# Cosine attention and a gated MLP on one core: AV turned round in batches 0 and 1, weights in larger packets, transfers held by waits

## The chip, the cores and the metric

The kernel runs on one core of a Trainium2 chip. Its metric is the device time of one execution in microseconds (us). A core has five engines that run their own instruction queues and meet through semaphores: TensorE (PE in the profile, with weight loads as PEld), VectorE (DVE), ScalarE (ACT), GpSimd (POOL) and SyncE (SP). Transfers are issued from the queues of SP, ACT and POOL and run on 16 DMA engines.

## The reference

Eight batches of 12 heads, 448 positions, head dimension 64, then an MLP from 768 over 2048 to 768 on the 3584 tokens; all in float32 at the kernel's borders.

```python
q_n = q / (norm(q) + 1e-6);  k_n = k / (norm(k) + 1e-6)
scores = q_n @ k_n.T / tau                       # tau = 0.1
attn = exp(scores - max(scores));  attn /= sum(attn) + 1e-9
x = (attn @ v) -> [tokens, heads * dim]
h = x @ w_in
out = (h * sigmoid(1.702 * h)) @ w_out
```

## The kernel before, in words

Heads go in pairs x: pair x belongs to batch x // 6, so that 0 to 5 are batch 0 and 6 to 11 batch 1; 48 pairs in all. Positions lie as 112 partitions by 4 chunks. For each pair q, k and v are loaded by SP (`load`, line 186, three transfers of 224 KB with 1 KB packets), ACT squares q and k (`square`, 193), DVE adds the squares up (`reduce`, 199) and turns the sums of a group of pairs into reciprocal norms (`norm_a`, `norm_b`, 212 to 240), POOL multiplies q and k with them and casts to fp16 (`scale`, 249), and v is cast with a column of ones beside it that makes the softmax denominators (`cast_v`, 262 or 264).

q and k must then lie with the head dimension on partitions. In batch 0 TensorE transposes them into PSUM and DVE copies them out (`transposes`, 271; `transposed`, 280); in the other batches a DMA transpose on SP does it (`dma_transposed`, 285).

Scores come with keys on partitions and queries along the row (`scores`, 297, and `scores_h`, 345, for half of the queries), ACT takes exp (`exp`, 308). AV has v as the stationary operand, with queries along the row and head dimension plus denominator on partitions (`attend`, 316; `attend_h`, 357). In batches 1 to 7 DVE evicts it (`attended`, 333), and for three pairs at a time the denominators go through DRAM to 112 partitions, are inverted on DVE (435), and come back spread over 64 partitions (`den_out` 423, `den_in` 430, `rcp_out` 440, `rcp_in` 445), for `normalise` (456). These transfers are issued by SP, but in batch 1 by ACT (`den_q`). Batch 0 takes halves of the queries instead: ACT evicts AV (`attended_h`, 367), TensorE picks the denominators onto partitions (`den_turn`, 375), DVE inverts them (386), TensorE spreads them (`den_spread`, 392), and DVE multiplies (`normalise_h`, 406).

The MLP of a batch starts when its six pairs are normalised: products with w_in (`mm1`, 467; for the halves of batch 0 `mm1_h`, 497), tanh on ACT (477), the gate on DVE (484; 509), products with w_out (`mm2`, 522), eviction on ACT (533), stores by SP (550). w_in and w_out come by two transfers each from POOL, which cast to fp16: w_in in halves of the columns (`load_w_in`, 558: 4 KB packets read), w_out in halves of the columns, too (`load_w_out`, 564: 1.5 KB packets read).

The order on each engine is not written by hand. Each step is an operation with an engine, an estimated duration, a due time, the operations it follows, and slots that it takes and frees (buffers, PSUM banks, and a "port" that keeps POOL apart from some DVE steps). `Plan.order` simulates the engines and the transfers with these and takes, on an idle engine, the ready operation that is due first; the instructions are issued in the order found. The semaphore waits come from the data alone. The due time of pair x is x in batch 0 and 2 x later. Loads of batch 1 follow scores or AV of batch 0 in the plan, w_in follows the load of q of pair 5, and w_out follows w_in. Slots: five q and five k buffers, three of v, one PSUM bank "a" (transposes and AV), two double banks for scores, three "mm" banks (MLP, and the denominators of batch 0).

Of the kernel before, what the change touches and what calls it, by code (L numbers as in the profile page):

```python
# [24 lines left out]
DMA_BYTES_PER_US = 250e3  # L25
MOE_FROM, MOE_LAG = 8, 9


class Plan:
# [3 lines left out]
    def __init__(self, slots):  # L33
        self.ops, self.free = {}, dict(slots)

    def add(self, name, eng, us, due, emit, after=(), takes=(), frees=(), nbytes=None, rows=128):
        self.ops[name] = (eng, us, due, emit, after, takes, frees, nbytes, rows)

    def order(self):
        ops = list(self.ops.values())  # L40
# [14 lines left out]
        while True:  # L55
            for e in idle:
                held = []
                while idle[e] <= now and ready[e]:
                    due, i = heapq.heappop(ready[e])
                    _, us, _, emit, _, takes, _, nbytes, rows = ops[i]  # L60
# [11 lines left out]
                    if nbytes is None:  # L72
                        heapq.heappush(events, (idle[e] + SEM_US, i, False))
# [5 lines left out]
            while True:  # L79
                heads = [q[0] for q in lines.values() if q]  # L80
                rate = DMA_BYTES_PER_US / max(len(heads), 1)
                landed = moved + min((h[0] for h in heads), default=0.0) / rate if heads else None
                if landed is None or (events and events[0][0] <= landed):
                    break
                for h in heads:
                    h[0] -= (landed - moved) * rate
                moved = landed
                for q in lines.values():
                    if q and q[0][0] <= 1e-3:
                        heapq.heappush(events, (moved + DMA_US + SEM_US, q.pop(0)[1], False))  # L90
# [3 lines left out]
            for h in heads:  # L94
                h[0] -= (now - moved) * rate
            moved = now
            while events and events[0][0] <= now:
                _, i, own = heapq.heappop(events)
                eng, nbytes = ops[i][0], ops[i][7]
                if own and nbytes is not None:  # L100
                    lines.setdefault(eng, []).append([nbytes, i])
                for s, k in ops[i][6]:
                    if own == (s == "port"):
                        self.free[s] += k
                for u in users[i]:
                    if (ops[u][0] == eng and nbytes is None) != own:
# [7 lines left out]
def kernel(  # L114
# [20 lines left out]
    NV = 6  # L135
    SH = S // 2
# [13 lines left out]
    p_in = pool("p_in", 5)  # L150
    p_v = pool("p_v", 3)
# [6 lines left out]
    p_ah = pool("p_ah", 2)  # L158
# [15 lines left out]
    pick = const.tile([128, 2], FP16)  # L174
# [8 lines left out]
    def load(x, d, src, nm):  # L183
        b, h0 = x // HP, (x % HP) * 2
        d[x] = p_in.tile([P, 2, C, D], FP32, name=nm)
        nc.sync.dma_start(
# [3 lines left out]

    def square(x, ti):
        sqs[x, ti] = p_sq.tile([P, 2, C, D], FP32, name="sq")
        nc.scalar.activation(out=sqs[x, ti], in_=(q32, k32)[ti][x], func=AF.Square)  # L193
# [39 lines left out]
    def norm_b(grp):  # L233
# [6 lines left out]
        nc.vector.tensor_tensor(out=y, in0=y, in1=t, op=ALU.mult)  # L240
# [4 lines left out]
    def scale(x, ti, eng=None):  # L245
# [3 lines left out]
        (eng or nc.gpsimd).tensor_tensor(  # L249
# [6 lines left out]
    def cast_v(x):  # L256
        src = v32.pop(x)
        vt = vts[x % NV]
        for j in range(2):
            dst = vt[:, :, j, 64 * j : 64 * j + D]  # L260
            if x < HP:
                nc.scalar.copy(out=dst, in_=src[:, j])
            else:
                nc.gpsimd.tensor_copy(out=dst, in_=src[:, j])  # L264
# [26 lines left out]
    tpss, exps, avs, sps, avps = {}, {}, {}, {}, {}  # L291
# [60 lines left out]

    def attend_h(x, h):
        ps = avps[x, h] = ps_a.tile([128, 2, SH], FP32, name="avh", tag="a")
        for j in range(2):
            for c in range(C):
                nc.tensor.matmul(  # L357
                    out=ps[:, j],
                    lhsT=vts[x % NV][:, c, j],
                    rhs=exps[x, h, c // 2][:, j, (c % 2) * SH : (c % 2 + 1) * SH],  # L360
                    start=(c == 0),
                    stop=(c == C - 1),
                )

    def attended_h(x, h):
        avs[x, h] = p_ah.tile([128, 2, SH], FP16, name="avsh")
        nc.scalar.activation(
            out=avs[x, h], in_=avps.pop((x, h)), func=AF.Copy, scale=AV_SCALE
        )

    def den_turn(x, h):
        ps = dps[x, h] = ps_m.tile([128, 512], FP32, name="mm")
        for i in range(2):
            for j in range(2):
                nc.tensor.matmul(
                    out=ps[:P, 2 * i + j : 2 * i + j + 1],
                    lhsT=avs[x, h][:, j, i * P : (i + 1) * P],
                    rhs=pick[:, j : j + 1],
                    start=True,
                    stop=True,  # L380
                )

    def den_rcp_h(x, h):
        r = dnms[x, h] = p_rc.tile([P, 4], FP16, name="rch")
        with nc.allow_low_precision("fp16 reciprocal of softmax denom"):
            nc.vector.reciprocal(out=r, in_=dps[x, h][:P, :4])

    def den_spread(x, h):
        r = dnms.pop((x, h))
        for i in range(2):  # L390
            for j in range(2):
                nc.tensor.matmul(
                    out=dps[x, h][64 * j : 64 * (j + 1), 64 + i * P : 64 + (i + 1) * P],
                    lhsT=r[:, 2 * i + j : 2 * i + j + 1].to_broadcast((P, 64)),
                    rhs=ident[:P, :P],
                    start=True,
# [399 lines left out]
```

## Time and profile before

| | |
|---|---|
| median of 3 runs | 505.68 us (505.25 to 506.33) |
| profiled execution | 505.82 us, of it the profile's span 503.9 us |
| TensorE busy | 464.0 us, 92% of the span, 2768 matmuls |
| ACT busy | 315.8 us, 63% |
| DVE busy | 279.2 us, 55% |
| POOL busy | 132.8 us, 26% |
| moved by DMA | 65.51 MB in 89902 packets, mean 130 GB/s |

The share of busy time is a mean over stages with different limits, and a matmul's busy time is longer when the clock granted to TensorE is lower. So a stage is read by its own windows: busy time of each engine, the granted clock beside it, and what the wait was for. The chain that ended last is the sequence of work that set the end, each piece with its start and length; where it passes from one engine to a DMA and back, the engines stood.

### The profile page before, as it was taken

The numbers are of one execution on the slowest core, as the hardware profiler recorded it, in microseconds if no ns is written. First come the engines' busy times: TensorE is split into PE (matmuls) and PEld (weight loads), VectorE is DVE, ScalarE is ACT, GpSimd is POOL, SyncE is SP. The second block draws the span as 40 slices with busy tenths as digits, with TensorE's granted clock in tenths as the row PEclk, the third lists the DMA queues.
The fourth block names the chain that finished last, engine by engine and source line by source line (L and its number), as shares of the span: only waits on it lengthen the run. The fifth ranks groups of instructions, "written<-read, shape, count | busy, mean of one in ns | idle before, by whom it ended". The sixth has DMA issues, their size and how long they took to land.

```text
span 503.9 us, 7803 instructions
## 1 busy us (share of the span) xinstructions
PE 464.0 (92%) x2768; PEld 248.1 (49%) x2768; DVE 279.2 (55%) x656; ACT 315.8 (63%) x497; POOL 132.8 (26%) x189
## 2 busy tenths in 40 slices
PE   0789889579699999999999999999999999999996
PEld 0566668325244455544544455445544554455553
DVE  7856476155476755396647745685468413641500
ACT  5968577283669765787668756786677545533411
POOL 1540525023426150515051505142503300000000
PEclk9999999858799999999999999999999999999999
DMA  9993819949268536755665365917570513012012
GB/s 225 237 234 103 205 34 156 223 116 224 62 181 196 152 68 188 150 163 97 183 166 145 73 154 141 243 36 201 132 178 24 132 33 91 2 60 64 0 40 86
DMA packets 89902, 65.51 MB, mean 130 GB/s; under 512 B 46388, under 2 KB 83080, under 8 KB 89864
## 3 DMA queue, kind: packets, MB, share of 16 engines
q1 hardware_dynamic: 83312, 58.02, 46.2%
q0 software_dynamic: 5696, 6.29, 7.8%
q10 hardware_dynamic: 856, 0.72, 0.5%
q8 instruction: 21, 0.34, 0.3%
q14 instruction: 17, 0.14, 0.1%
HBM read 50.51 MB, written 11.16 MB: 122 GB/s over the span
## 4 chain that ended last, share of the span: by engine, by line
PE 74%; DVE 7%; DMA 7%; ACT 5%; issue 3%; SPq 1%; POOL 1%; ACTq 0%; POOLq 0%; DVEq 0%
PE mm L522 26%; PE mm L467 22%; PE avp L316 11%; PE sp L297 6%; DMA q<-in_q_dram 3%; PE avh L357 3%; PE mm L497 3%; ACT expT L308 2%; PE sp L345 2%; DMA k<-in_k_dram 2%; ACT sq L193 1%; DMA den<-av 1%; DVE n L199 1%; DVE xT L456 1%; POOL qks L249 1%
## 5 line engine op out<-in xcount | busy, mean ns | idle before, releaser
L308 ACT ACTIVATE expT<-sp 112x896 f16<-112x896 f32 x192 | 166.5, 915 | 65.5 <-PE sp L297 57.4
L522 PE MATMUL mm<-w_out,gT 128*128 128x384 f16 x896 | 154.4, 329 | 0.0
L467 PE MATMUL mm<-xT,w_in 128*128 128x448 f16 x672 | 134.3, 353 | 1.2 <-DVE gT L484 1.1
L522 PEld LDWEIGHTS <-gT 128*128 128x128 f16 x896 | 85.6, 98 | 66.5 <-issue 13.0
L484 DVE SCALAR_TENSOR_TENSOR gT<-th,mm 128x448 f16<-128x448 f16 x112 | 67.9, 618 | 57.1 <-ACT th L477 56.6
L477 ACT ACTIVATE th<-mm 128x448 f16<-128x448 f32 x128 | 69.1, 545 | 45.8 <-PE mm L467 29.7
L467 PEld LDWEIGHTS <-w_in 128*128 128x128 f16 x672 | 63.0, 98 | 67.8 <-issue 13.0
L249 POOL TENSOR_TENSOR qks<-k,y 112x512 f16<-112x512 f32 x48 | 50.5, 1053 | 146.2 <-issue 101.6
L333 DVE TENSOR_SCALAR av<-avp 65x448 f16<-65x448 f32 x84 | 51.9, 618 | 62.6 <-PE avp L316 62.5
L316 PE MATMUL avp<-expT,vt 112*128 112x448 f16 x336 | 82.0, 366 | 1.6 <-DVE av L333 1.3
L199 DVE TENSOR_REDUCE n<-sq 112x8 f32<-112x512 f32 x96 | 63.7, 679 | 29.9 <-ACT sq L193 29.5
L297 PE MATMUL sp<-qkT 64*112 64x448 f16 x336 | 54.3, 388 | 13.7 <-ACT expT L308 13.6
L264 POOL CAST vt<-v 112x256 f16<-112x256 f32 x84 | 32.4, 417 | 116.9 <-DMA v<-in_v_dram 99.0
L533 ACT ACTIVATE ost<-mm 128x384 f32<-128x384 f32 x56 | 27.3, 490 | 51.9 <-PE mm L522 50.4
L249 POOL TENSOR_TENSOR qks<-q,y 112x512 f16<-112x512 f32 x47 | 49.0, 1042 | 0.0
L316 PEld LDWEIGHTS <-vt 112*128 112x128 f16 x336 | 32.7, 99 | 32.9 <-issue 6.7
L297 PEld LDWEIGHTS <-qkT 64*112 64x112 f16 x336 | 17.1, 129 | 49.7 <-issue 47.1
L456 DVE TENSOR_TENSOR xT<-av,rcb 64x448 f16<-64x448 f16 x84 | 34.5, 411 | 7.0 <-DMA rcb<-rcp 5.7
L193 ACT ACTIVATE sq<-k 112x512 f32<-112x512 f32 x48 | 30.2, 630 | 10.6 <-DMA k<-in_k_dram 6.6
L193 ACT ACTIVATE sq<-q 112x512 f32<-112x512 f32 x48 | 30.3, 632 | 2.9 <-DVE n L199 1.6
L497 PE MATMUL mm<-xT,w_in 128*128 128x224 f16 x192 | 21.7, 273 | 0.0
L497 PEld LDWEIGHTS <-w_in 128*128 128x128 f16 x192 | 19.1, 104 | 2.4 <-issue 1.6
(41 smaller groups left out, 171.4 us busy)
## 6 DMA issues: line engine op xcount, KB each, us to landing
k<-in_k_dram SPq DMA_DIRECT2D x48, 224.0 KB
q<-in_q_dram SPq DMA_DIRECT2D x48, 224.0 KB
v<-in_v_dram SPq DMA_DIRECT2D x48, 224.0 KB
rcb<-rcp SPq DMA_DIRECT2D x24, 168.0 KB
w_in<-in_moe_w_in_dram POOLq DMA_DIRECT2D x2, 1536.0 KB, 17.4
w_out<-in_moe_w_out_dram POOLq DMA_DIRECT2D x2, 1536.0 KB, 21.4
out_dram<-ost SPq DMA_DIRECT2D x7, 336.0 KB
out_dram<-ost SPq DMA_DIRECT2D x8, 288.0 KB
```

The lines of the kernel that those rows point to most:

```text
L193: nc.scalar.activation(out=sqs[x, ti], in_=(q32, k32)[ti][x], func=AF.Square)
L199: nc.vector.tensor_reduce(out=n2s[grp][:, x - grp[0], ti], in_=sqs.pop((x, ti)), axis=AX.X, op=ALU.add,)
L249: (eng or nc.gpsimd).tensor_tensor(out=qkss[x][:, ti].rearrange("p c j d -> p j c d"), in0=src, in1=rss[x][:, ti, :, :, None].to_broadcast ...
L297: nc.tensor.matmul(out=sp[:, j, :S], lhsT=qkT[64 * j : 64 * (j + 1), 1, c * P : (c + 1) * P], rhs=qkT[64 * j : 64 * (j + 1), 0, :], start= ...
L308: nc.scalar.activation(out=e, in_=sps.pop(key)[:, :, :S], func=AF.Exp, scale=inv_tau, **kw)
L316: nc.tensor.matmul(out=ps, lhsT=vts[x % NV][:, c, j], rhs=exps[x, c][:, j], start=(c == 0), stop=(c == C - 1),)
L333: nc.vector.tensor_scalar(out=avs[x][:n, j], in0=ps[:n], scalar1=AV_SCALE, scalar2=None, op0=ALU.mult)
L467: nc.tensor.matmul(out=ps[:, :S], lhsT=w_in_sb[:, kk, 128 * m : 128 * (m + 1)], rhs=xTs[b, kk], start=(kk == 0), stop=(kk == KT1 - 1),)
L477: nc.scalar.activation(out=ths[key], in_=mms[key][:, :S], func=AF.Tanh, scale=0.851)
L484: nc.vector.scalar_tensor_tensor(out=gts[b // 2][:, m, (b % 2) * S : (b % 2 + 1) * S], in0=ths.pop((b, m)), scalar=1.0, in1=mms.pop((b, m) ...
L497: nc.tensor.matmul(out=ps[:, i * SH : (i + 1) * SH], lhsT=w_in_sb[:, kk, 128 * (m + i) : 128 * (m + i + 1)], rhs=xTs[0, kk][:, h * SH : (h ...
L522: nc.tensor.matmul(out=mms[b2, t, n][:, :NW], lhsT=gts[b2][:, kk, 128 * t : 128 * (t + 1)], rhs=w_out_sb[:, kk, NW * n : NW * (n + 1)], st ...
```

## The change

In batches 0 and 1 the exponentials become the stationary operand of AV and v the moving one, so that queries lie on partitions and the denominator is a column; DVE inverts and multiplies there, TensorE transposes the result back, and a copy (ACT for the first halves of batch 0, else DVE) writes it for the MLP. Batch 1 takes the half-query path that was batch 0's. The denominators' DMAs are left to batches 2 to 7, all on SP. Batch 1's squares go from ACT to POOL. w_out is split by rows instead of columns (3 KB packets read); w_in is as before.

Loads get a fixed order among themselves ("turns": sorted by due time, one issued after the other), and some wait for others to land, by semaphores that the plan adds (`hold`): w_in for q of pair 4; q, k and v of pairs 6 to 8 for the first half of w_in, of 9 to 11 for the second; w_out for q of pair 11; q, k and v of pair 12 for the second half of w_out. POOL operations that take the port wait for the DVE operation that had it last. The plan's model of a transfer counts packets and their sizes. Norm groups of batch 0 are (0), (1, 2), (3, 4, 5), those of batch 1 are of two pairs; due times of squares, norms and transposes are earlier by 1 to 4; there are seven q and seven k buffers and four of v; the second halves of batch 0 wait in the plan for the first halves of pairs three later. The copy of q of pair 0 is issued by ACT.

```diff
+    def emit(self, link):
+        names, done, port = list(self.ops), {}, None
+        for _, i, emit in self.order():
+            eng, takes, hold = self.ops[names[i]][0], self.ops[names[i]][5], self.ops[names[i]][9]
+            insts = emit()
...
+            for h in hold:
+                link(insts[0], done[h])
+            if ("port", 1) in takes:
+                if eng == "DVE":
+                    port = insts[-1]
+                elif port is not None:
+                    link(insts[0], port)
...
     def square(x, ti):
-        nc.scalar.activation(out=sqs[x, ti], in_=(q32, k32)[ti][x], func=AF.Square)
+        src = (q32, k32)[ti][x]
+        if on_pool(x, ti):
+            return nc.gpsimd.tensor_tensor(out=sqs[x, ti], in0=src, in1=src, op=ALU.mult)
+        return nc.scalar.activation(out=sqs[x, ti], in_=src, func=AF.Square)
...
     def attend_h(x, h):
+        ps = avps[x, h] = ps_m.tile([128, 512], FP32, name="mm")
         for i in range(2):
             for j in range(2):
+                o = 132 * i + 65 * j
+                for c in range(C):
+                    at = (c % 2) * SH + i * P
+                    nc.tensor.matmul(
+                        out=ps[:P, o : o + D + 1],
+                        lhsT=exps[x, h, c // 2][:, j, at : at + P],
+                        rhs=vts[x % NV][:, c, j, 63 * j : 63 * j + D + 1],
+                        start=(c == 0),
+                        stop=(c == C - 1),
+                    )
+
+    def normalise_h(x, h):
+        ps = avps[x, h][:P, :264].rearrange("p (i e) -> p i e", i=2)
+        r = p_rc.tile([P, 2, 2], FP32, name="rch")
+        nc.vector.reciprocal(out=r, in_=ps[:, :, D : D + 2])
+        xss[x, h] = p_xs.tile([P, 2, 2, D], FP16, name="xs")
+        nc.vector.tensor_tensor(
+            out=xss[x, h],
+            in0=ps.rearrange("p i (j e) -> p i j e", j=2)[:, :, :, :D],
+            in1=r[:, :, :, None].to_broadcast((P, 2, 2, D)),
+            op=ALU.mult,
+        )
+
+    def turn_h(x, h):
+        ps, xs = avps[x, h][:, 384:].bitcast(FP16), xss.pop((x, h))
         for i in range(2):
+            nc.tensor.transpose(
+                out=ps[:, i * P : (i + 1) * P],
+                in_=xs[:, i].rearrange("p j d -> p (j d)"),
+                identity=ident[:P, :P],
+            )
+
+    def turned_h(x, h):
...
+        (nc.scalar.copy if b + h == 0 else nc.vector.tensor_copy)(
+            out=xTs[b, hp][:, h * SH : (h + 1) * SH],
+            in_=avps.pop((x, h))[:, 384:].bitcast(FP16)[:, :SH],
+        )
...
-    def load_w_out(n):
-        cols = slice(NW * n, NW * (n + 1))
-        nc.gpsimd.dma_start(
-            out=w_out_sb[:, :, cols],
-            in_=moe_w_out.rearrange("(k p) n -> p k n", p=128)[:, :, cols],
+    def load_w_out(i):
+        k = slice(8 * i, 8 * (i + 1))
+        return nc.gpsimd.dma_start(
+            out=w_out_sb[:, k], in_=moe_w_out.rearrange("(k p) n -> p k n", p=128)[:, k]
         )
...
+        hold = [("w_in", int(x >= HP + 3))] if HP <= x < 2 * HP else [("w_out", 1)] if x == 2 * HP else []
...
-        add(("w_in", i), "POOL", 1.0, 2 * i - 2, partial(load_w_in, i), after=[("load", "q", HP - 1)],
-            nbytes=3.14e6, **port)
-        add(("w_out", i), "POOL", 1.0, 11 + 2 * i, partial(load_w_out, i), after=[("w_in", 1)], nbytes=3.14e6, **port)
+        add(("w_in", i), "POOL", 1.0, i - 2, partial(load_w_in, i), hold=[("load", "q", HP - 2)],
+            dma=packets(768, 4096), **port)
+        add(("w_out", i), "POOL", 1.0, 9 + i, partial(load_w_out, i), hold=[("load", "q", 2 * HP - 1)],
+            dma=packets(1024, 3072), **port)
```

More of the change, by code (lines that the diff above doesn't have):

```diff
@@ L258, in cast_v @@
         vt = vts[x % NV]
[L259 to L264, printed above, removed]
+        copy = nc.scalar.copy if x < HP else nc.gpsimd.tensor_copy
+        return tuple(
+            copy(out=vt[:, :, j, 64 * j : 64 * j + D], in_=src[:, j]) for j in range(2)
+        )
     def transposes(x):
@@ L353, in attend_h @@
     def attend_h(x, h):
[L354 to L369, printed above, removed]
```

243 lines of the change are left out of this document (114 added, 129 removed).

## The prediction

> **What bounds the kernel now.** I read first the windows of the span, then the chain that ended last, the waits, and last the DMA rows of the two stretches in which the chain leaves TensorE.
>
> ```profile
> span 503.9 us, 7803 instructions
> 11.00:60.00 49.00, 40.67 (x298) 28.85 (x299) 32.93 (x88) 37.46 (x63) 20.21 (x25) 1.00 0.86 193
> 60.00:90.00 30.00, 28.70 (x253) 22.16 (x252) 19.16 (x44) 22.16 (x35) 10.45 (x14) 1.00 0.75 118
> 90.00:100.00 10.00, 4.50 (x37) 2.96 (x35) 1.15 (x2) 1.12 (x2) 0.74 (x2) 0.84 1.24 225
> 100.00:110.00 10.00, 6.22 (x18) 1.89 (x18) 5.11 (x14) 7.03 (x10) 0.74 (x2) 0.50 0.63 162
> 110.00:120.00 10.00, 9.61 (x37) 4.20 (x37) 4.19 (x10) 6.12 (x10) 7.41 (x10) 0.63 0.70 149
> 120.00:130.00 10.00, 7.06 (x43) 3.68 (x41) 5.82 (x13) 3.88 (x6) 0.00 (x0) 1.00 0.55 141
> 130.00:140.00 10.00, 8.66 (x32) 2.81 (x32) 4.93 (x16) 7.14 (x10) 6.96 (x9) 0.66 0.44 113
> 150.00:480.00 330.00, 328.73 (x1877) 164.30 (x1876) 189.44 (x412) 215.17 (x340) 82.53 (x118) 1.00 0.47 118
> ```
>
> After the window come its length and the busy time of PE, weight loads, DVE, ACT and POOL, then granted clock, DMA share and GB/s. From 150 us on TensorE is busy 328.73 of 330 us at full clock: nothing is to be gained there except by less TensorE work. The loss lies before. Busy time times clock, from 90 to 140 us, is 4.50 x 0.84 + 6.22 x 0.50 + 9.61 x 0.63 + 7.06 + 8.66 x 0.66 = 25.7 us of work in 50 us: **24.3 us lost**. From 60 to 90 only 1.3 us are lost. From 11 to 60 the clock column says 1.00, but the chain of waits disagrees:
>
> ```profile
> 30.52 0.28 PE mm L375 x4
> 30.80 0.55 PE sp L345 x4
> 31.35 0.33 PE mm L392 x4
> ...
> 34.18 1.65 PE avh L357 x8
> 35.83 0.92 PE sp L345 x6
> 36.75 0.46 PE mm L375 x4
> ...
> 63.52 0.87 PE avh L357 x8
> ...
> 86.94 12.83 DMA q<-in_q_dram
> ...
> 99.85 1.35 DMA den<-av
> ```
>
> The same eight AV matmuls take 1.65 us at 34 us and 0.87 us at 63 us: TensorE runs at about half speed until the dense products of batch 0's MLP begin (line 497, next fence). So the 40.67 us of busy time up to 60 are worth about 40.67 x 0.87 / 1.65 = 21.4 us: **27.6 us lost**, the larger part by clock.
>
> The second loss begins with a DMA. The first rows below are from the waits, the rest from the instructions in order of time and from the DMA rows of the weight transfers.
>
> ```profile
> PE sp L297 <- ACT expT L308: 13.6, 10, 8.1
> ACT th L477 <- DMA den<-av: 9.5, 1, 9.5
> ...
> L497 PE MATMUL mm<-xT,w_in x192: 256/259/394, 59.0 to 94.2; 128*128 128x224 f16 x192
> ...
> 60.35 0.45 SPq L186 DMA_DIRECT2D v<-in_v_dram  x1
> ...
> 74.30 2.36 POOL L564 DMA_DIRECT2D w_out<-in_moe_w_out_dram  x2
> ...
> 85.21 0.91 SPq L186 DMA_DIRECT2D v<-in_v_dram  x1
> ...
> DMA to landing us min/median/max: 15.7/21.4/27.2
> ```
>
> ACT's queue holds a DMA issue of its own (denominators of batch 1), which stands until a q load issued at 86.94 has landed 12.83 us later, and tanh and exp stand behind it for 9.5 us; TensorE then waits 8.1 us for an exp and comes back at half clock. The q load is slow because it shares the engines with w_out, issued at 74.3 and needing 15.7 and 27.2 us to land; between SP's loads at 60.35 and 85.21 only transposes are issued. Which link ties ACT's issue to a q load the trace does not say; that it does is in the chain.
>
> **The change part by part.** *Denominators off ACT's queue, w_out ahead of batch 2's loads.* In batches 0 and 1 no denominator goes through a DMA any more, and the other batches' go by SP; ACT keeps a single DMA issue, q of pair 0. The 9.5 us wait has nothing to stand on. w_out is held until q of pair 11 has landed, and k of pair 12 until w_out's second half has. Prices, from DMA rows of 16 to 41 us (w_in) and of 74 to 103 us (w_out), two groups of ACT and the page's rate by slice:
>
> ```profile
> q0 software_dynamic: 1568, 3.15, 67.5%
> q0 software_dynamic: 4128, 3.15, 76.9%
> ...
> L308 ACT ACTIVATE expT<-sp 112x896 f16<-112x896 f32 x24 | 21.1, 915 | 5.6 <-PE sp L345 5.5
> ...
> L477 ACT ACTIVATE th<-mm 128x448 f16<-128x448 f32 x128 | 69.1, 545 | 45.8 <-PE mm L467 29.7
> ...
> GB/s 225 237 234 103 205 34 156 223 116 224 62 181 196 152 68 188 150 163 97 183 166 145 73 154 141 243 36 201 132 178 24 132 33 91 2 60 64 0 40 86
> ```
>
> That is 25 x 0.675 = 16.9 us of all engines for w_in and 29 x 0.769 = 22.3 us for w_out. Half as many packets of twice the size bring w_out towards w_in's price; I take 18.5, between the two. Loads of batch 1 no longer run beside w_in. A load of 224 KB at the first slices' 234 GB/s takes 0.98 us, so q of pair 4, the eleventh, lands at about 13; w_in issues then and, with the eight loads left beside it, lands by about 38, the last nine loads of batch 1 to q of pair 11 by about 47, w_out by about 66, instead of 74.3 + 1.2 + 27.2 = 102.7 now (the second half's issue comes 1.2 after the first's). Batch 2's loads then follow an empty queue. What is late next: batch 1's attention, which needs ACT: 24 exps of 0.915 us, 16 tanh of batch 0 at 0.545 and six evictions at about the same, some 34 us from about 49 to 85. I leave 6 us of loss in place of 24.3, an estimate; its bounds are 1.3 (the windows 60 to 90) and 24.3. **Gain 18 us** (0 to 23).
>
> *Batch 0's AV with queries on partitions.* Before, one half of a pair puts on the half-speed chain 2 x 0.55 of scores, 1.65 of AV, 0.46 and 0.33 of the two denominator steps: 3.5 us. After, AV is sixteen matmuls of 65 columns, each with its own weights of 112 columns, and the two later steps are two transposes. The nearest rows are L375's loads of 112 columns with a single column to multiply, one set at half clock, one at full:
>
> ```profile
> 18.02 0.49 PEld L375 LDWEIGHTS <-avsh 128*112 128x112 f16 x4
> 67.02 0.28 PEld L375 LDWEIGHTS <-avsh 128*112 128x112 f16 x4
> ...
> L375 PEld LDWEIGHTS <-avsh x12: 126/131/132, 65.3 to 69.0; 128*112 128x112 f16 x12
> L375 PEld LDWEIGHTS <-avsh 128*112 128x112 f16 x36 | 4.3, 205 | 3.3 <-ACT avsh L367 2.9 <-issue 0.3
> ...
> 183.34 0.76 PE avp L316 x4
> ```
>
> Less the last one's own duration, the spacing is (0.49 - 0.205) / 3 = 0.095 and (0.28 - 0.131) / 3 = 0.050 us. The 65 columns are fewer than the 112 loaded, so I let the load set the pace: AV 16 x 0.095 = 1.52 at half clock, 0.80 at full. With 0.2 for two transposes at the same spacing the half of a pair costs 2.8 instead of 3.5: twelve times 0.7 is 8.4 us. If load and matmul did not overlap at all, 0.095 x (112 + 65) / 112 = 0.15 each, 2.4 us, and this gain would turn into a loss of 0.2 us each; the present AV at 1.65 / 8 = 0.206 for 224 columns hides its loads, which is why I take the first.
>
> The Trainium skill, "TensorE: Matmul & The Clock Gate", section "LDWEIGHTS (loading the stationary operand)", puts a load at its columns divided by 1.2 GHz, 93 ns for 112. That agrees with the half-clock rows and not with the 50 ns at full clock; by it AV would stay at 1.5 us there, and the sum would be the rival's that is priced at 95 ns below.
>
> The AV results now go to one of three "mm" banks instead of the single bank shared with the transposes, so a pair's AV need not wait for the previous eviction. The first normalisation no longer queues behind other pairs' reductions, and GpSimd's scaling waits for VectorE's norm, whose steps it now slows:
>
> ```profile
> 23.71 0.18 DVE L225 SCALAR_TENSOR_TENSOR t<-y 112x16 f32<-112x16 f32 x1
> ...
> 25.95 0.97 DVE L225 SCALAR_TENSOR_TENSOR t<-y 112x16 f32<-112x16 f32 x1
> ```
>
> Four such steps at 0.97 instead of 0.18 us cost 3.2 us. Behind the waiting GpSimd stand its scalings, casts and weight issues; the wait is at most one norm. With all first halves of batch 0 done near 38 us and w_in there, the MLP's dense products start some 20 us before 59.0, and the last third of batch 0's attention runs at full clock: four halves at about 1.5 less, 6 us. 8.4 + 6 + 3.2 is 17.6, but the other engines cap it:
>
> ```profile
> L367 ACT ACTIVATE avsh<-avh 128x448 f16<-128x448 f32 x10 | 5.4, 542 | 6.0 <-PE avh L357 5.7
> L193 ACT ACTIVATE sq<-k 112x512 f32<-112x512 f32 x9 | 5.7, 629 | 0.0
> ```
>
> In these 49 us ACT is busy 37.46. It loses the 5.4 us of avsh and most squares of batch 1 (at least six of 0.63), and gains six copies of about 0.5: some 31 us remain, and at an assumed 85% they need 37. VectorE's 32.93 less 3.2 need 35 by the same share. **Gain 12 us** (0 to 17).
>
> *Batch 1's AV at full clock.* Now eight matmuls of 0.19 us a pair (0.76 for four, the last row of the fence on L375), 1.5 us; after, 32 x 0.050 and four transposes taken at the same, 1.8 us: **0.3 x 6 = 2 us more**, on TensorE's path, for there it binds. With VectorE nothing changes much: two evictions and two multiplications a pair go, a reciprocal, a multiplication and a copy for each half come.
>
> ```profile
> L249 POOL TENSOR_TENSOR qks<-k,y 112x512 f16<-112x512 f32 x48 | 50.5, 1053 | 146.2 <-issue 101.6 <-DVE y L240 23.0 <-DVE rch L386 17.9
> ```
>
> The squares of batch 1 on GpSimd are twelve of 1.05 us (its scalings of the same shape), 12.6 us beside 10.45 + 20.21 busy in 79 us: hidden; without that cover they would delay batch 1's attention by as much. The wait of w_out stands on GpSimd's queue ahead of batch 1's last scalings, which need the same loads anyway.
>
> The sum against the profiled execution, 505.8 us (the span and 1.9 around it; the median of the runs shown is 505.7): 505.8 - 18 - 12 + 2 = **477.8, say 478 us**.
>
> **The rivals.** *Only one stage gains.* Batch 0's stage is paced by ACT and by the half clock as before, and only the stall at 95 goes: 505.8 - 18 + 2 = 490 (485 to 495). For it: ACT busy 37 of 49 us and VectorE at 33 leave little slack. Against: the chain in that stage is mostly TensorE.
>
> *Both stages nearly clean.* 17 and 23 gained: 468, with 8 us less, 460, if the rest of the half-clock loss went too. For it: from 60 to 90 the same mixture of work loses 1.3 us. Against: ACT's 34 us in batch 1.
>
> *Weight loads at 95 ns at full clock too.* 24 halves x 16 x 0.045 = 17 us more TensorE work: 495. Against: the row at 67.02.
>
> *Slower: SP parked behind w_out.* SP takes its loads in a strict order, in which v of pair 11 stands behind k and q of pair 12, and these wait for w_out's second half. If w_out lands late, pair 11's AV and so batch 1's MLP wait for it while TensorE has nothing else past about 85 us. The time is then 478 + (landing - 85), slower than now from a landing at about 113 on; with 27.2 us to land as now, that means w_out issued only at about 86, twelve later than now. At 120 it would be 513. For it: three chained holds, each a landing that the order only estimated. Against: less traffic beside each.
>
> *The change does not do what it says*: the planner's order comes out the same and the holds hold nothing: 505.8. The new AV alone makes that unlikely.
>
> **How the numbers follow.** Forecast 0.50, one stage only 0.25, both clean 0.11, loads at 95 ns 0.05, SP parked 0.07 (0.06 of it slower), nothing 0.02. The range, 462 to 495, holds the first four cases except their edges, some 0.85. Two runs of this kernel can tell apart about 0.2%, 1 us; faster by more 0.92, within it 0.02, slower 0.06. The forecast's own range is 469 to 485.
>
> **What would show it.** Right: the first dense product (line of mm1_h) near 38 us and not 59; no wait of ACT on a DMA near 95; w_out landed near 66; granted clock 1.00 from about 42 on without the dips at 97 and 131; the first full-width product of batch 1 near 120, not 150.8; AV matmuls of 65 columns at 50 ns spacing. Wrong: w_out landing past 85 with SP idle at a load, ACT over 90% busy from 15 to 85 with TensorE waiting on exp, or AV at 95 ns after 60 us.

## The result, and the profile after

The changed kernel takes 488.43 us (median of four runs, 487.54 to 492.81) against 505.47 us for four runs of the kernel before beside them: a ratio of 0.968, 95% interval 0.962 to 0.975. The forecast was 478, the range 462 to 495. The time fell into the band of the rival "Only one stage gains" (485 to 495), and the traces say much the same: the second stage is nearly clean, the first gained half or less of what was forecast.

The profiled execution took 487.54 us. These are its windows, with the columns explained in the prediction (length; busy PE, weight loads, DVE, ACT, POOL; clock; DMA share; GB/s).

```profile
span 485.7 us, 8249 instructions
...
11.00:60.00 49.00, 41.70 (x388) 32.66 (x386) 29.12 (x81) 31.12 (x53) 25.80 (x27) 1.00 0.87 191
60.00:90.00 30.00, 24.83 (x308) 22.30 (x307) 18.26 (x57) 17.31 (x25) 16.53 (x23) 0.94 1.02 189
90.00:100.00 10.00, 10.00 (x118) 7.48 (x117) 7.67 (x20) 9.21 (x16) 1.50 (x4) 1.00 1.12 268
100.00:110.00 10.00, 9.61 (x102) 6.70 (x101) 8.99 (x26) 8.56 (x16) 7.94 (x12) 1.00 0.73 175
110.00:120.00 10.00, 10.00 (x60) 4.43 (x58) 7.20 (x22) 9.80 (x15) 6.94 (x9) 1.00 1.01 269
120.00:130.00 10.00, 10.00 (x58) 4.55 (x56) 6.82 (x16) 9.91 (x16) 7.83 (x11) 1.00 1.17 256
130.00:140.00 10.00, 10.00 (x56) 4.50 (x55) 6.93 (x18) 9.14 (x15) 2.59 (x5) 1.00 0.87 241
150.00:480.00 330.00, 324.61 (x1866) 165.16 (x1865) 176.83 (x365) 196.18 (x309) 70.53 (x97) 1.00 0.40 101
```

Lost time again as length less busy time times clock. From 90 to 140 it is now 0.4 us and was 24.3. From 60 to 90 it is 30 - 24.83 x 0.94 = 6.7, and was 1.3. Together 25.6 became 7.1: **18.5 us gained between 60 and 140**. From 150 to 480 5.4 us are lost instead of 1.3, **4.1 given back**. The two profiled executions differ by 18.3, so what is left for the start and the stage up to 60 is 18.3 - 18.5 + 4.1 = **3.9 us**, where the prediction had 12. Lost time does not count that batch 1's new AV is more work for TensorE; with the 1.8 us that the rows give for it (next section but one), the first stage gained 5.7.

The chain that ended last (start, length, what):

```profile
32.50 1.63 PE mm L402 x16
...
44.90 0.30 PE mm L425 x2
...
48.07 2.35 PE mm L521 x12
...
64.04 2.05 POOL qks L291 x2
66.12 13.47 DMA qkT<-qks
79.64 0.87 PE sp L385 x8
...
83.95 0.10 PE mm L425 x2
84.05 0.81 PE mm L402 x16
```

Line 402 is the new AV, 425 the two transposes of its result, 521 the dense product of halves, 385 the scores of halves. Sixteen AV matmuls take 1.63 us at half clock and 0.81 at full. The dense products begin at 48.0, not at 59.0 and not at the forecast's 38; the clock record goes to full at 52.5 (62.8 before), once more to half from 79.8 to 83.2, and stays full after that. The first full-width product of batch 1 is at 125.7 instead of 150.8.

Three views follow: the waits from 55 to 85 us (engine, line, what it waited for: us in all, times, longest); how long w_out's two transfers took; and GpSimd in order of time (start, length, operation, idle time before it and what ended that).

```profile
PEld L385 <- DMA qkT<-qks: 5.2, 1, 5.2
...
POOL w_out L588 <- DVE xT L435: 4.6, 1, 4.6
```

```profile
DMA to landing us min/median/max: 12.8/14.6/16.4
```

```profile
16.16 0.83 POOL L582 DMA_DIRECT2D w_in<-in_moe_w_in_dram  x1 [1.31 <-DVE y L281]
17.00 1.05 POOL L291 TENSOR_TENSOR qks<-k,y 112x512 f16<-112x512 f32 x1
...
57.58 0.94 POOL L588 DMA_DIRECT2D w_out<-in_moe_w_out_dram  x1
63.15 0.88 POOL L588 DMA_DIRECT2D w_out<-in_moe_w_out_dram  x1 [4.62 <-DVE xT L435]
```

ACT no longer waits for a DMA of the denominators. A new wait stands at 70 to 80: TensorE idles some 5 us for a DMA transpose of batch 1 that was issued at 66.12, beside the second half of w_out, and took 13.47 us. w_out's second half landed at 63.15 + 16.4 = 79.5, not at 66, and the transpose ended with it (66.12 + 13.47 = 79.6).

### The profile page after: what moved, and what is told of

The parts are those of the page before. It is cut to its first block, busy times and chain, and to the rows that moved or that the text cites. A ratio compares the mean times of both kernels' runs of the same rounds, so it can differ in the third digit from the quotient of the medians.

```text
span 485.7 us, 8249 instructions
## 1 busy us (share of the span) xinstructions
PE 452.7 (93%) x3008; PEld 253.5 (52%) x3008; DVE 278.3 (57%) x657; ACT 304.8 (63%) x479; POOL 147.2 (30%) x201
## 4 chain that ended last, share of the span: by engine, by line
PE 72%; DMA 12%; DVE 6%; SPq 4%; issue 2%; ACT 2%; POOL 2%; ACTq 0%; POOLq 0%; DVEq 0%
PE mm L546 28%; PE mm L491 18%; PE avp L356 8%; PE sp L337 6%; PE mm L402 4%; PE sp L385 3%; PE mm L521 3%; DMA qkT<-qks 3%; DMA k<-in_k_dram 2%; DMA q<-in_q_dram 2%; SPq L221 2%; DMA dnm<-den 2%; DMA v<-in_v_dram 2%; DVE xT L480 2%; POOL qks L291 1%
## 5 line engine op out<-in xcount | busy, mean ns | idle before, releaser
L491 PEld LDWEIGHTS <-w_in 128*128 128x128 f16 x672 | 63.1, 98 | 70.7 <-issue 16.0
L373 DVE TENSOR_SCALAR av<-avp 65x448 f16<-65x448 f32 x72 | 44.4, 616 | 48.9 <-PE avp L356 48.6
L356 PE MATMUL avp<-expT,vt 112*128 112x448 f16 x288 | 66.4, 352 | 1.4 <-DVE av L373 1.4
L337 PE MATMUL sp<-qkT 64*112 64x448 f16 x288 | 43.0, 372 | 0.0
L356 PEld LDWEIGHTS <-vt 112*128 112x128 f16 x288 | 27.9, 97 | 26.4 <-issue 2.0
L234 ACT ACTIVATE sq<-k 112x512 f32<-112x512 f32 x42 | 26.5, 634 | 16.1 <-DMA k<-in_k_dram 14.6
L402 PE MATMUL mm<-vt,expT 112*112 112x65 f16 x384 | 30.9, 242 | 3.0 <-ACT expT L348 2.7
L402 PEld LDWEIGHTS <-expT 112*112 112x112 f16 x384 | 28.7, 161 | 6.3 <-ACT expT L348 3.7
L234 ACT ACTIVATE sq<-q 112x512 f32<-112x512 f32 x42 | 26.4, 633 | 7.7 <-DVE n L240 5.1
L385 PE MATMUL sp<-qkT 64*112 64x224 f16 x192 | 20.6, 325 | 8.1 <-DMA qkT<-qks 4.9
```

Of the source, the lines that this page charges most:

```text
L234: return nc.scalar.activation(out=sqs[x, ti], in_=src, func=AF.Square)
L337: nc.tensor.matmul(out=sp[:, j, :S], lhsT=qkT[64 * j : 64 * (j + 1), 1, c * P : (c + 1) * P], rhs=qkT[64 * j : 64 * (j + 1), 0, :], start= ...
L356: nc.tensor.matmul(out=ps, lhsT=vts[x % NV][:, c, j], rhs=exps[x, c][:, j], start=(c == 0), stop=(c == C - 1),)
L402: nc.tensor.matmul(out=ps[:P, o : o + D + 1], lhsT=exps[x, h, c // 2][:, j, at : at + P], rhs=vts[x % NV][:, c, j, 63 * j : 63 * j + D + 1 ...
L491: nc.tensor.matmul(out=ps[:, :S], lhsT=w_in_sb[:, kk, 128 * m : 128 * (m + 1)], rhs=xTs[b, kk], start=(kk == 0), stop=(kk == KT1 - 1),)
```

## The experiments

Each ratio is to runs of the kernel before (medians 504.9 to 505.4 us) on the same chip, with its 95% interval. The theory at the start was that of the prediction: the second stage gains because ACT's queue is free and w_out comes early. Its rivals: the packets, the held waits, the squares on GpSimd, or the new AV path in batch 1. A second question was the hole at 70 to 80, that is, TensorE's idle time there, and a third why batch 0's stage gained so little. The planner orders all engines anew when an estimate or an operation changes. So all runs but a_nolink, a_noport and a_warm show their edit together with a new order.

**1. The denominators' issues alone (b_den_sp).** The kernel before, batch 1's denominators on SP:

```diff
     def den_q(g):
-        return nc.scalar if g * GRP // HP == 1 else nc.sync
+        return nc.sync
...
-        dq = "ACT" if x // HP == 1 else "SP"
+        dq = "SP"
```

> The kernel before with one edit: the denominators of batch 1 are issued by SP, as those of the other batches, so that ACT issues no DMA. Theory (the stall at 95 us comes from ACT's queue standing at its own DMA issue): the 9.5 us wait of ACT goes, TensorE no longer stands 8.1 us, the dip of the granted clock at 97 us goes; about 490 to 497 us, a gain of 9 to 16. Rival (the stall comes from w_out sharing the engines with batch 2's loads and batch 1's transposes, whoever issues): the wait turns up elsewhere, 502 to 508 us.

Measured: 502.37 us, 0.9943 (0.9924 to 0.9962). Its windows:

```profile
90.00:100.00 10.00, 7.60 (x52) 4.16 (x51) 5.36 (x9) 7.39 (x12) 0.75 (x2) 1.00 1.23 238
100.00:110.00 10.00, 8.70 (x34) 3.69 (x34) 4.92 (x14) 5.34 (x9) 7.69 (x11) 0.66 0.89 216
...
120.00:130.00 10.00, 8.14 (x32) 3.34 (x32) 6.68 (x18) 6.37 (x9) 7.30 (x9) 0.66 0.81 181
```

The wait that the prediction was built on is gone (7.60 busy at full clock where it was 4.50 at 0.84), and the half clock has only moved: it now begins at 71.0, 101.7 and 122.2. The chain still runs through the slow load of q (from 85.96, 12.59 us long), now to a square on ACT instead of a DMA issue. The end comes 3 us earlier. The wait that the profile named last was real; behind it stood the next one. ACT's issue alone is worth 3 us.

**2. AV alone (b_newav).** The kernel before with nothing but the new attend_h, normalise_h, turn_h and turned_h in batches 0 and 1 (`HALF = 2 * HP`); loads, weights, squares, groups and due times as before.

> The kernel before with the new AV, normalisation and turning back in batches 0 and 1 alone: no holds, no turns, weights in the packets of before, squares on ACT, buffers and norm groups as before. Theory (the new AV of batch 1 is enough for most of the gain): 488 to 495 us. Rival (it needs w_out ahead of batch 2's loads, which still collide here at 74 to 103 us): 499 to 506 us, with TensorE waiting from 94 on.

Measured: 497.89 us, 0.9862 (0.9813 to 0.9912), between the two expectations. Its window from 60 to 90 and the rows of its w_out:

```profile
60.00:90.00 30.00, 26.06 (x233) 21.70 (x232) 14.95 (x43) 17.15 (x24) 10.44 (x14) 0.66 0.84 144
```

```profile
L550 POOL DMA_DIRECT2D w_out<-in_moe_w_out_dram x2: 1147/1178/1210, 75.9 to 77.1; - x2
...
DMA to landing us min/median/max: 17.0/20.6/24.1
```

Seven of the 17 us come with AV alone. w_out still lands at 77.1 + 24.1 = 101 us, the first product with it is at 110.7 (93.8 in the changed kernel), and much of 60 to 90 goes at half clock.

**3 and 4. Everything but batch 1's AV (a_half6, a_half6_g2).** The changed kernel with batch 1 back on whole queries, so that its denominators travel through DRAM again, by SP: `HALF = HP`. That one edit also made the norm groups of batch 1 threes; the second kernel has pairs as in the changed kernel.

```diff
-    HALF = 2 * HP
+    HALF = HP
```
```diff
-    groups += [tuple(range(g, g + 2)) for g in range(HP, HALF, 2)]
-    groups += [tuple(range(g, g + GRP)) for g in range(HALF, NPAIR, GRP)]
+    groups += [tuple(range(g, g + 2)) for g in range(HP, 2 * HP, 2)]
+    groups += [tuple(range(g, g + GRP)) for g in range(2 * HP, NPAIR, GRP)]
```

> The changed kernel with batch 1 taken back to whole queries: v stationary in AV, two evictions on VectorE, denominators through DMAs, all on SP, groups of three for its norms; batch 0, the holds, the packets and the squares on GpSimd stay. Theory (the second stage gains mainly because w_out comes early and in order, not by the new AV of batch 1): 486 to 491 us, with about 2 us less TensorE work at full clock and a little more waiting. Rival (batch 1's own path without denominator DMAs is what closes the stage from 90 to 140 us): 495 to 502 us, TensorE waiting between 90 and 140.

> As the kernel with batch 1 on whole queries and denominators through DMAs (509.6 us), but with its norms in groups of two pairs as in the changed kernel. Theory (the 21 us that batch 1's new AV is worth are the round trip of the denominators, from the last AV of batch 1 to its first full-width product, when TensorE has nothing else): 500 to 510 us, TensorE still waiting about 10 us or more between 110 and 150. Rival (what cost the time there was the later start of batch 1's scores with norm groups of three): 486 to 493 us.

Measured: 509.63 us, 1.0081 (1.0055 to 1.0106), slower than both expectations, and with pairs 504.15, 0.9978 (0.9953 to 1.0002), inside its theory's range. So all the rest of the change, batch 0's new AV among it, is worth nothing without batch 1's. For a_half6 the windows, the waits from 90 to 150, VectorE and GpSimd in order of time, and SP's queue:

```profile
120.00:130.00 10.00, 4.63 (x26) 1.96 (x25) 6.42 (x17) 6.47 (x11) 5.52 (x9) 0.94 1.09 217
130.00:140.00 10.00, 4.20 (x13) 1.27 (x13) 8.22 (x12) 3.06 (x5) 6.26 (x8) 0.50 0.85 210
```

```profile
PE avp L356 <- DVE av L373: 11.5, 4, 10.4
```

```profile
128.09 6.13 DVE L480 TENSOR_TENSOR xT<-av,rcb 64x448 f16<-64x448 f16 x6
134.25 0.30 DVE L459 RECIPROCAL rcg<-dnm 112x24 f16<-112x24 f16 x1
134.47 0.56 DVE L373 TENSOR_SCALAR av<-avp 65x448 f16<-65x448 f32 x1
...
146.82 2.43 DVE L480 TENSOR_TENSOR xT<-av,rcb 64x448 f16<-64x448 f16 x6
```

```profile
129.34 1.19 POOL L291 TENSOR_TENSOR qks<-q,y 112x512 f16<-112x512 f32 x1
130.49 1.19 POOL L291 TENSOR_TENSOR qks<-k,y 112x512 f16<-112x512 f32 x1
```

```profile
122.37 0.67 SPq L447 DMA_DIRECT2D den<-av  x1
...
128.51 0.41 SPq L454 DMA_DIRECT2D dnm<-den  x1
...
134.58 0.32 SPq L464 DMA_DIRECT2D rcp<-rcg  x1
...
137.67 1.18 SPq L469 DMA_DIRECT2D rcb<-rcp  x2
```

Two things lie in this hole. The denominators of pairs 9 to 11 leave at 122.4 and come back with the transfer issued at 137.7, and the multiplications that use them start at 146.8; the dense products of batch 1 begin only at 148.7, as late as before (150.8). And on VectorE six multiplications of the group before take 1.02 us each (6.13 / 6; 0.41 each at 146.82) beside a row of GpSimd scalings, with an AV eviction behind them for which TensorE waits 10.4 us. With pairs the same hole is there (dense products at 146.9, a wait of 7.6 us for that eviction). The new AV path has neither the transfers nor these multiplications in batch 1. How the hole divides between the two was not tried.

**5 to 7. Packets, held waits, squares (a_cols, a_nolink, a_sqact).** The changed kernel with w_out by column halves in 1.5 KB packets as before; with the added semaphore waits left out but the same order; with batch 1's squares on ACT. The first also takes the plan's price of the smaller packets, and the products with w_out wait for the column half that they need.

```diff
-        k = slice(8 * i, 8 * (i + 1))
+        cols = slice(NW * i, NW * (i + 1))
```
```diff
             for h in hold:
-                link(insts[0], done[h])
+                pass
```
```diff
-        return x // HP == 1
+        return False
```

> The changed kernel with w_out by halves of the columns as before (1.5 KB packets read), the plan's price of it changed with it. Theory (the order and the moment of w_out matter, its packets cost 3 to 5 us of landing at most): 488 to 492 us. Rival (the smaller packets are what choked the transposes and loads beside them): 495 us or more.

> The changed kernel without the added waits of transfers for other transfers to land; the order on every queue is the same, only the semaphore waits go. Theory (the order alone puts w_in and w_out in their place, since SP's and GpSimd's queues hold them behind other waits): 486 to 491 us. Rival (without the holds batch 1's loads run beside w_in and batch 2's beside w_out, as before the change, and TensorE waits again): 493 to 503 us.

> The changed kernel with batch 1's squares on ACT, as before, in place of GpSimd. Theory (GpSimd is full between 35 and 70 us and its order delays batch 1's scaling and w_out's issue, 57.6 us, ten after q of pair 11 has landed, while ACT is busy 60%): 482 to 487 us. Rival (ACT paces batch 1's attention): 489 to 495 us.

Measured: 488.45, 488.20 and 488.15 us; 0.9658 (0.9628 to 0.9689), 0.9661 (0.9634 to 0.9689), 0.9661 (0.9614 to 0.9707). None differs from the changed kernel's 488.43. w_out in small packets needed 19.9 us for its second half instead of 16.4, which landed at 81.4, before the first product with it at 89.8. Without the held waits w_in's first issue is at 10.5 instead of 13.8, but GpSimd then waits 4.6 us for the port, the second issue stays at 16.1 and the end where it was: given this order, the waits add nothing. With the squares on ACT w_out goes at 55.1 and 56.0 and the hole at 70 to 80 shrinks to 1 us; the time lies between the two expectations. In a_cols the hole shrinks to 1.3 us as well. In neither does the end come earlier: with the squares on ACT TensorE idles 4.5 us from 140 to 150 and falls to half clock at 147.9; in a_cols 1.6 us are lost there, and 330 - 323.42 x 0.99 = 9.8 instead of 5.4 from 150 to 480.

So what the changed kernel has beyond AV alone is worth some 9 us (ratios of 0.986 and 0.968), and taking out any one of these three parts costs nothing of it. The waits for the port come next. What then remains is mainly the fixed order of the loads, the norm groups, the due times and the buffers, and these were not tried one by one.

**8. The waits for the port (a_noport).**

```diff
                 elif port is not None:
-                    link(insts[0], port)
+                    pass
```

> The changed kernel without the added waits of GpSimd for the VectorE operation that last had the port; order and all else the same. Theory (they hold w_out's second half, 57.6 to 63.2 us, and batch 1's scaling behind it): w_out's second half issued at about 59, the gap of TensorE shorter by 2 to 4 us, 484 to 487 us. Rival (they keep VectorE's norm steps from running at 0.97 us): steps of 0.97 us come back, batch 0's first products later by 2 to 4 us, 489 to 493 us.

Measured: 486.70 us, 0.9618 (0.9592 to 0.9644), which overlaps the changed kernel's interval: inconclusive. w_out's halves go at 55.7 and 56.7, so the port did hold the second one, but the hole at 70 to 80 is still there (TensorE busy 5.21 of 10 us). VectorE's norm steps before 25 us stay at 0.2 us but for one of 0.49, so the rival fails.

**9. The hole at 70 to 80 (a_tp1).** Batch 1's q and k turned on TensorE, as in batch 0, instead of by DMA:

```diff
-        if first:
+        if x < HALF:
             add(("tp", x), "PE", 0.4, s - 3, partial(transposes, x),
```

> The changed kernel with batch 1's q and k turned by TensorE and copied by VectorE, as batch 0's are, in place of DMA transposes on SP. Theory (TensorE's idle time from 72 to 80 us is one DMA transpose of 13.5 us that shares the engines with w_out): that gap goes, no dip of the clock at 80, 480 to 485 us. Rival (ACT or VectorE is next in that place): the gap closes by less than half, 486 to 490 us.

Measured: 483.62 us, 0.9574 (0.9551 to 0.9596). The window 70 to 80 of the changed kernel, and then of this one:

```profile
70.00:80.00 10.00, 5.10 (x66) 4.60 (x65) 5.37 (x18) 3.71 (x6) 5.86 (x10) 0.99 1.20 184
```

```profile
70.00:80.00 10.00, 9.62 (x130) 8.97 (x131) 7.65 (x26) 6.98 (x10) 7.67 (x13) 1.00 0.82 164
```

The idle time and the half clock after it are gone, and the end comes 4.8 us earlier. So the DMA transpose beside w_out caused the hole. That the hole by itself was worth these 4.8 us is not shown: in a_cols and a_sqact it shrinks too, and as much is lost elsewhere.

**10 and 11. The half clock of batch 0 (a_warm, a_tp1_warm2).** Matmuls whose results are overwritten: 28 of 512 columns before the first transposes, and 4 ahead of each AV of batch 0; in the second kernel, on a_tp1, 28 and 2.

```diff
         ps = avps[x, h] = ps_m.tile([128, 512], FP32, name="mm")
+        for _ in range(4 if x < HP else 0):
+            nc.tensor.matmul(out=ps, lhsT=warm[:, :128], rhs=warm, start=True, stop=True)
```

> The changed kernel with extra matmuls of ones whose results are overwritten: 28 of 512 columns before the first transposes, and four ahead of each AV of batch 0 in the same PSUM bank; the output's arithmetic is unchanged. Theory (batch 0's stage lost what the prediction promised because TensorE stays at half clock until 52 us): clock at full from about 5 us on, the first dense product from 48 to about 38 to 42, 479 to 484 us. Rival (the stage is paced by ACT, VectorE and loads): the first dense product within 2 us of 48 and 486 to 493 us.

> The changed kernel with batch 1 turned by TensorE (483.6 us alone) and extra matmuls of ones whose results are overwritten: 28 before the first transposes, and two ahead of each AV of batch 0 (four put 12 us of their own on the chain before). Theory (half clock is what batch 0's stage still loses): granted clock full for most of 15 to 47 us, the first dense product at 42 to 45 us, 478 to 482 us. Rival (GpSimd's scaling and the order of halves pace it): the first dense product at 46 to 48, 482 to 486 us.

Measured: 488.59 us, 0.9669 (0.9634 to 0.9703), and 488.14, 0.9663 (0.9614 to 0.9712). The chain of a_warm, where line 398 is the added work and 404 AV, and then that of a_tp1_warm2:

```profile
23.06 1.82 PE mm L398 x4
24.88 1.47 PE mm L404 x16
...
33.42 0.97 PE mm L398 x4
34.38 0.81 PE mm L404 x16
```

```profile
33.44 0.97 PE mm L398 x2
34.41 1.46 PE mm L404 x16
```

The 28 matmuls raised the clock for about 10 us (6.0 to 16.2, and 5.9 to 16.1). Four before each AV brought it to full again at 29.9, and AV there to 0.81 us; but each four cost 0.97 us on TensorE's own path, and the dense products began at 46.9 instead of 48.0. a_warm came out as its rival said, though a full clock was there from 29.9 on. Two left the clock at half until 57.1, the dense products began at 52.3, and the end came 4.5 us after that of a_tp1, later than both expectations. In a_warm the end shows no gain: the clock seems to have paid for the added work and no more. No run has this stage at full clock without such work.

**12. The best of these together (a_tp1_np_sq).** Batch 1 turned on TensorE, its squares on ACT, the weights' issues free of the port.

```diff
-        return x // HP == 1
+        return False
...
-        if first:
+        if x < HALF:
...
-            dma=packets(768, 4096), **port)
+            dma=packets(768, 4096))
...
-            dma=packets(1024, 3072), **port)
+            dma=packets(1024, 3072))
```

> A version put together: batch 1 turned by TensorE, its squares on ACT, and the weights' issues without the port in the plan, so that they wait for no VectorE operation. Theory (w_in's second issue delays the scaling of pairs 1 and 2 by about 1 us and w_out's second by 5): first dense product 1 to 2 us earlier, w_out's second half issued within 2 us of the first, 479 to 483 us. Rival (with the gap after 70 us gone, ACT paces the stage to 110 us and squares there cost): 484 to 488 us.

Measured: 482.73 us, 0.9553 (0.951 to 0.9596), the lowest here, though its interval overlaps that of a_tp1. Dense products begin at 44.0, 3.6 us before those of a_tp1, and the scaling of pair 1 at 15.84 instead of 16.69; little of that reaches the end.

## Why the prediction was right or wrong

The measured time lies in the range, but nearer to a rival than to the forecast. Of the two stages one came out at its size for another reason than the one given, and the other fell short.

**The price of the new AV: right.** 0.81 us for sixteen at full clock (0.80 said), 1.46 to 1.64 at half (1.52). Their loads hide. That refutes the rival of 95 ns at full clock. The Trainium skill, "TensorE: Matmul & The Clock Gate", section "LDWEIGHTS (loading the stationary operand)", has 93 ns for 112 columns; that holds here at half clock alone (1.63 / 16 = 0.102 with the matmul), and at full clock the measured 0.81 / 16 = 0.051 decides.

**The second stage, 18 us: the size was right, the step behind it wrong.** The step was "Denominators off ACT's queue, w_out ahead of batch 2's loads". Its price was a wait of ACT, while batch 1's new AV was booked as 2 us of cost. ACT's queue alone is worth 3 us (b_den_sp), and it is this AV on which the gain hangs: with batch 1 on its old path, its denominators on SP's queue and the order otherwise that of the changed kernel, the time is 504 to 510. There the round trip through DRAM and VectorE's slow multiplications hold batch 1's dense products back about as long as before (to 148.7 and 146.9, 150.8 before); which of them weighs more is open. AV alone gives 7, the rest alone 0 to -5, both 17. The two need each other. The 6 us of loss left were an estimate without a sum, so that the stage came to 18.5 is partly luck. The prediction costed no packets, holds or squares as gains of their own, and taken out one at a time they change nothing. With AV alone w_out lands at 101 and batch 0's second products begin 17 us later than in the changed kernel (that w_out alone sets this is not shown); with the order alone batch 1's MLP waits for its denominators.

**w_out near 66: wrong, 79.5.** The load that holds it was down for 47 and q of pair 11 landed at 48.4. But w_out was issued at 57.6 and 63.2, behind squares and scalings of batch 1 on GpSimd's queue, the second half after 4.6 us of wait for the port. The prediction had w_out standing ahead of batch 1's last scalings at no cost. It stands behind the four scalings of the first two pairs and ahead of the other eight, and the chain runs through it: from its second issue at 63.15 to the scalings at 64.04 and the slow transpose at 66.12. The transfer itself was priced at 18.5 for both halves and took 21.9, from 57.6 to 79.5, with 5.6 between the issues.

**Loss left in the second stage, 6 us: right in size (7.1 from 60 to 140), for another cause.** The prediction put it down to ACT; 5 us of it are the DMA transpose (a_tp1). The prediction knew that loads beside w_out are slow, and did not ask what would run beside w_out once it came earlier.

**Batch 0's stage, 12 us: the step that failed; about 4 to 6 came.** The step was "With all first halves of batch 0 done near 38 us and w_in there, the MLP's dense products start". No sum stands behind the 38. The copies of the first halves on ACT show when they were done:

```profile
40.49 0.34 ACT L435 COPY xT<-mm 128x224 f16<-128x224 f16 x1
45.82 0.34 ACT L435 COPY xT<-mm 128x224 f16<-128x224 f16 x1
```

The sixth and last was done at 46.2, and the dense products began at 48.0. In the order found two second halves stand ahead of it, so that eight halves of AV had to run first (ten in the kernel before); by 38 us five had been started, and four before. Its three terms:

- *8.4 us, at 0.7 a half.* AV and its two transposes take 1.46 to 1.64 and 0.30 us at half clock, against 1.65, 0.46 and 0.33 before: 0.5 to 0.7 less, so the term is right or a little high. But from the second AV (23.8) to the eighth (45.9) a half took 22.0 / 6 = 3.7 us and not 2.8, because the transposes of q and k (three times 0.9 us) and TensorE's waits (1.4 us in all) stand on the same path, and the price of a half left them out.
- *3.2 us for the first norms.* The norm steps at 21 to 25 us did fall to 0.2 us, but attention starts hardly earlier: GpSimd now stands at w_in for q of pair 4 (3.4 us) and for the port (1.31), pair 1 is scaled at 17.00 instead of 14.30, and the second AV starts at 23.8 instead of 24.1.
- *6 us for an early clock.* They shrank, since full clock came at 52.5 and not at 42, after the dense products had begun, as in all kernels without added matmuls (last section).

The caps on ACT and VectorE did not act: ACT was busy 31.12 of 49 us, as computed, and TensorE 41.70. That GpSimd's waits set the late start is argued from these rows. The kernel that eased them and also moved the squares (a_tp1_np_sq) began its dense products 3.6 us before a_tp1 and ended 0.9 us earlier, which the intervals do not separate.

**Batch 1 at 2 us more: right by the rows.** A pair now takes 2 x (0.81 + 0.10) = 1.8 us, as said, against 1.5 before; 1.8 us in all for six pairs. No run separates it in the time.

**After 150: 4.1 us, not foreseen.** The prediction took the steady part as fixed. TensorE now waits there 3.9 us for the gate and 1.4 for an AV eviction, both on VectorE (last section).

**SP parked behind w_out** did not happen: w_out landed at 79.5, before the 85 from which it would have cost.

## What to carry to other kernels

The wait that ends a stall last is not what the stall is worth: move it alone and see whether the time falls or the next wait steps in. A part that gives nothing alone may be needed for another's gain, so test both each alone and each left out. And when a bulk transfer is moved earlier, look which small transfers on the critical path will now run beside it.

## What the runs showed of the hardware

**A transpose by DMA beside a bulk cast load took 13.47 us**, and ended when that load had landed. From 150 us on the profile gives a median of 2.9 us for such a transpose. The one for which TensorE waited ended at 79.6, w_out's second half landed at 79.5; in a_noport both are at 78.4, in a_nolink at 79.3 and 79.2, in a_sqact at 76.0 and 75.8, in a_cols both at 81.4 (another transpose came through there at 74.7). In a_noport, with w_out issued earlier, the transpose took 14.46 us, so its length is no fixed price. Why it waits no run here shows.

**A VectorE multiplication of 64x448 fp16 takes 0.39 us, and 1.02 beside a GpSimd scaling of 1.19 (1.04 alone).** Both plans keep the two apart, by estimated times; in the changed kernel GpSimd also waits for VectorE's last step with the port, but VectorE does not wait for GpSimd, and in the execution they meet more often. The Trainium skill, "SBUF — State Buffer", section "Who interferes with whom", says that a VectorE step with two inputs in SBUF contends with a GpSimd step that reads SBUF; the trace agrees, and shows VectorE near GpSimd's pace (1.02 us, against a scaling every 1.15) for as long as GpSimd's row of scalings lasts. The multiplications of the kernel before (min/median/max ns), and of the changed one:

```profile
L456 DVE TENSOR_TENSOR xT<-av,rcb x84: 373/389/628, 123.7 to 452.5; 64x448 f16<-64x448 f16 x84
```

```profile
L480 DVE TENSOR_TENSOR xT<-av,rcb x72: 376/389/1237, 147.7 to 434.4; 64x448 f16<-64x448 f16 x72
```

In the steady part of the changed kernel six of them take 4.84 us, and a dense product then waits for the gate behind them:

```profile
249.22 4.84 DVE L480 TENSOR_TENSOR xT<-av,rcb 64x448 f16<-64x448 f16 x6
254.10 1.15 DVE L508 SCALAR_TENSOR_TENSOR gT<-th,mm 128x448 f16<-128x448 f16 x2
...
254.77 2.43 PE L491 MATMUL mm<-xT,w_in 128*128 128x448 f16 x12 [2.06 <-DVE gT L508]
```

That is 2.06 of the 5.4 us lost after 150. No run takes it away: without the port's waits (a_noport) these multiplications have a mean of 499 ns, against 510.

**Busy is not enough for full clock.** From 40 to 52.5 TensorE had hardly a gap (19.75 of 20 us busy from 40 to 60), and the clock stayed at half. Up to 48.0 it ran scores, AV and transposes (64*112, 112*112 and 112*128 in the profile's rows); then the dense products began (128*128), and the clock was full 4.5 us later. In the twelve kernels without added matmuls it first became full 1.8 to 4.9 us after the first dense product (before: 59.0 and 62.8; a_tp1_np_sq: 44.0 and 46.4). In b_newav it fell back to half from 64.7 to 85.2, with TensorE busy 9.18 of 10 us on scores and AV from 70 to 80, and came back 4.6 us after dense products had begun at 80.66. Two added matmuls of 512 columns for every sixteen small ones did not raise it, four did. The Trainium skill, "TensorE: Matmul & The Clock Gate", section "What's actually happening", gives about 3.4 us of sustained activity; the times after the first dense product are near that, but 8 us of scores and AV from 40 on, and 10 from 70 on in b_newav, did not do, and the measurement decides. What the hardware counts as activity no run here shows.

The granted clock in the windows reads 1.00 until the first record of it; the AV matmuls, 1.63 us against 0.81, show the half clock there. So the 1.3 us lost from 60 to 90 in the kernel before leave out its half clock until 62.8, another 1.4 or so that belong to batch 0's stage.
